# Regrouping the products with V in a fused attention, routing and gated-convolution kernel

## The chip, the cores and the metric

The kernel runs on one core of one Trainium2 chip. The metric is device time in microseconds (us) of one execution; less is better. The engines named below are PE (TensorE: matmuls and transposes), ACT (ScalarE), DVE (VectorE), POOL (GpSimd) and SP (SyncE, which issues nearly all of the DMAs here). Each runs its own instructions in program order and waits for the others through semaphores.

## The reference, cut to what matters

Three stages follow each other. Only the first, clustered attention over 2 batches, 8 heads, 768 positions and 64 channels a head, is touched.

```python
def _attn_ref(q, k, v, centroids):
    scale = 1.0 / np.sqrt(D)
    q_assign = np.argmax(np.einsum('bhsd,hcd->bhsc', q_n, c_n), axis=-1)
    k_assign = np.argmax(np.einsum('bhsd,hcd->bhsc', k_n, c_n), axis=-1)
    mask = q_assign[:, :, :, None] == k_assign[:, :, None, :]
    scores = scale * np.matmul(q, k.transpose(0, 1, 3, 2))
    scores = np.where(mask, scores, -1000000000.0)
    scores = scores - np.max(scores, axis=-1, keepdims=True)
    attn = np.exp(scores)
    attn = attn / (np.sum(attn, axis=-1, keepdims=True) + 1e-09)
    return np.matmul(attn, v).astype(np.float32)
...
x = _moe_ref(x=x, **moe_kwargs)      # each token goes through one of 8 experts
return _moe2_ref(x=x, **moe2_kwargs) # causal convolution gate, value product, output product
```

## The kernel before, in words

The attention handles 8 pairs of heads (`g` 0 to 7). A pair has two query blocks of 384 queries (`u` counts the blocks, 0 to 15), and a block has six items: 3 tiles of 128 queries times 2 heads. So there are 96 items and one loop over them, written out in program order; this text calls one pass of it a **trip**, and counts the trips of a pair 0 to 11 (`i % 12`; `j` is 0 to 5 within a block). Nothing reorders the instructions: each engine does its share of each trip in the order of the code.

A trip `i` does, in this order:

- `do_S(i + 2)` (L658): four PE matmuls make the scores of item `i + 2` in one of the **two** buffers of `ps_s` (tile `s`), and DVE takes the row maximum (`mx`, L675). The buffer is the one that item `i` used, so these matmuls wait until ACT has read it, that is for the exponential of item `i`.
- `do_T(i)` (L689): six PE transposes of item `i`'s exponentials, in two halves (`tp`, two buffers), each copied to SBUF (`pt`). In the trips 2, 3, 4, 5, 6 and 9 of a pair ACT copies both halves (L704); in the others DVE copies one (L702).
- `do_exp(i + 2)` (L678): the exponential on ACT (L684), once the maximum is there.
- the **products with V** (`do_PV`, L706) of the block before: six key tiles, two matmuls each (one for each head, 64 columns wide), added up in `pv`. They come in groups of two key tiles, in the trips `j` = 1, 3 and 5. After the last, ACT copies `pv` (`post1`, L718).
- a step of the **preparation of the next pair** (`prep_steps`, L369). `k_hi` and `q_hi` (ACT), `k_lo` (POOL) and `q_lo` (DVE) split keys and queries into a high and a low part in tile `xx`; `dots1` (PE: `dott`, then DVE: `dsb`) and `dots2` (PE: `dots`) make the products with the cluster centres; `argmax1` to `argmax4` (DVE, POOL) find each position's cluster; `rows` (PE: `pr`) and `rows_out` (ACT: `ohr`) turn it into one-hot rows. `stack1` (three SP DMAs a head, `st<-xx`) and `stack2` (two a head, `st<-ohr`) lay it all into `st`, from which the scores of the next pair are made from trip 10 on. The list has six steps, done in the trips 0 to 5 of a pair; in the first pair (which prepares the second) in the trips 1 to 6.
- in `j` = 3 (`j` = 4 in the pairs 4 and 5) `post2` (L725) of the block before the last: three PE products (`po`) and four small DVE operations. In the pairs 4 and 5 the trips 6 to 9 also hold steps of the routing of tokens (`route_steps`, L518), with a scan on DVE (`r3`) between two PE steps (`r2p`, `r3p`).

The first block has no products with V, since there is no block before it, and the last block (`u` 15) does them in two groups of three already, in its first two trips. Trip 7 of the first pair also holds nine small DVE operations of `conv_weights`.

Of the kernel before, what the change touches and what calls it, by code (L numbers as in the profile page):

```python
# [8 lines left out]
F32 = mybir.dt.float32  # L9
# [32 lines left out]
def routed_attention_moe_kernel(  # L42
# [12 lines left out]
    nc = tc.nc  # L55
# [58 lines left out]
    def keep_warm(ps, n):  # L114

        for _ in range(n):
            nc.tensor.matmul(ps, onesb, onesb.unsqueeze(1).to_broadcast([128, 4, 128]), start=True, stop=True)
# [251 lines left out]
    def prep_steps(g):  # L369
        b, p = pairs[g]  # L370
        x = X[g]
        xx = xx_p.tile([128, 4, S], F32R, tag="xx", name="xx")
# [72 lines left out]
            nc.scalar.activation(ohr, pr, AF.Identity, bias=rowb[:, 1:2], scale=rowb[:, 0:1])  # L445
            o["ohr"] = ohr

        def stack1(h):
            s = st[h]
            r = slice(64 * h, 64 * h + 64)  # L450
            nc.sync.dma_start(s[0:64, 0:2, :].bitcast(F32), xx[r, 0:2, :].bitcast(F32))
            nc.sync.dma_start(s[64:128, 0:2, :].bitcast(F32), xx[r, 0:3:2, :].bitcast(F32))
            nc.sync.dma_start(s[0:64, 2:4, :].bitcast(F32), xx[r, 1:4:2, :].bitcast(F32))

        def stack2(h):
            r = o["ohr"].bitcast(F32)
            nc.sync.dma_start(st[h][64:80, 2, :].bitcast(F32), r[32 + 16 * h:48 + 16 * h, :])
            nc.sync.dma_start(st[h][64:80, 3, :].bitcast(F32), r[16 * h:16 * h + 16, :])

        def S0(h, parts=None):  # L460

            if parts:
                S_[h] = ps_s.tile([128, 2, 512], F32, tag="s", name="s")
                r = slice(64 * h, 64 * h + 64)
                for n, (a, c) in enumerate(parts):
                    for m in range(2):
                        nc.tensor.matmul(
                            S_[h][:, m, :384], xx[r, a, 0:128], xx[r, c, 384 * m:384 * m + 384],
                            start=(n == 0), stop=False,
                        )  # L470
            else:
                for m in range(2):
                    nc.tensor.matmul(
                        S_[h][:, m, :384], st[h][64:80, 2, 0:128], st[h][64:80, 3, 384 * m:384 * m + 384],
                        start=False, stop=True,
                    )
                row_max(h, S_[h])

        def rows0(h):
            for i in range(2):  # L480
                pl, tag = ((ps_t, "t"), (ps_v, "pv") if i else (ps_m, "m"))[h]
                pr = pl.tile([128, 1024], BF16, tag=tag, name="pr0")
                for t in range(NQT):
                    c = 8 * (t % 3) + 4 * (t // 3) + 2 * i + h
                    nc.tensor.transpose(pr[64:80, 128 * t:128 * t + 128], o["oh"][:, c, :], identb)
                if i:
                    nc.scalar.copy(st[h][64:80, 2, :], pr[64:80, :S])
                else:
                    nc.vector.tensor_scalar(
                        st[h][64:80, 3, :], pr[64:80, :S], NEG, -NEG, op0=ALU.mult, op1=ALU.add  # L490
                    )

        if g == 0:
            return [[
                cent_norm, k_hi, k_lo, q_hi, dots1, dots2, q_lo,
                lambda: nc.scalar.activation(warm[:, 1:2], warm[:, 0:1], AF.Exp),
                lambda: S0(0, ((1, 0), (1, 3), (2, 0))), lambda: S0(1, ((1, 0), (1, 3), (2, 0))),
                lambda: keep_warm(ps_v.tile([128, 512], F32, tag="pv", name="spin1"), 2),
                lambda: stack1(0), lambda: stack1(1),
                argmax1, argmax2, argmax3, argmax4, lambda: rows0(0), lambda: rows0(1), lambda: S0(0), lambda: S0(1),  # L500
            ]]
        return [
            [k_hi, dots1],
            [q_hi, k_lo, dots2],
            [argmax1, argmax2],
            [q_lo, lambda: stack1(0), lambda: stack1(1)],
            [argmax3, argmax4],
            [rows, rows_out, lambda: stack2(0), lambda: stack2(1)],
        ]

# [147 lines left out]
    def do_S(i):  # L658
        g, qb, t, h = items[i]
        st = ST[g][h]  # L660
        q0 = 384 * qb + 128 * t
        ps = ps_s.tile([128, 2, 512], F32, tag="s", name="s")
        for n in range(2):
            nc.tensor.matmul(  # L664
                ps[:, n, :384], st[:, 1, q0:q0 + 128], st[:, 0, 384 * n:384 * n + 384], start=True, stop=False
            )
        for n in range(2):
            nc.tensor.matmul(  # L668
                ps[:, n, :384], st[0:80, 2, q0:q0 + 128], st[0:80, 3, 384 * n:384 * n + 384], start=False, stop=True
            )  # L670
        row_max(i, ps)
# [6 lines left out]
    def do_exp(i):  # L678
        g, qb, t, h = items[i]
        ps, mx = S_.pop(i)  # L680
        if (t, h) == (0, 0):
            Zt[i // 6] = small.tile([128, 3, 2], F32, tag="z", name="z", bufs=4)
        pt = p_p.tile([128, 2, 384], F32, tag="p", name="pexp", bufs=3)
        nc.scalar.activation(  # L684
            pt, ps[:, :, :384], AF.Exp, bias=mx[:, 0:1], accum_out=Zt[i // 6][:, t, h:h + 1]
        )
        P_[i] = pt.rearrange("p a b -> p (a b)")

    def do_T(i, act_only):  # L689
        g, qb, t, h = items[i]  # L690
        u = i // 6
        if t == 0:
            PT[u, h] = pt_p.tile([128, NQT, 384], F32, tag=f"pt{h}", name=f"pt{h}")
        p = P_.pop(i)
        for half in range(2):
            tp = ps_t.tile([128, 3, 128], F32, tag="t", name="tp")
            for k in range(3):
                kt = 3 * half + k
                nc.tensor.transpose(tp[:, k, :], p[:, 128 * kt:128 * kt + 128], ident)  # L699
            dst = PT[u, h][:, 3 * half:3 * half + 3, 128 * t:128 * t + 128]  # L700
            if half == 0 and not act_only:
                nc.vector.tensor_copy(dst, tp)  # L702
            else:
                nc.scalar.copy(dst, tp)  # L704

    def do_PV(u, kt):  # L706
        g, qb = items[6 * u][:2]
        if kt == 0:
            PVs[u] = ps_v.tile([128, 384], F32, tag="pv", name="pv")
        for h in range(2):  # L710
            nc.tensor.matmul(  # L711
                PVs[u][64 * h:64 * h + 64, :], Vt[g][:, kt, h, :], PT[u, h][:, kt, :],
                start=(kt == 0), stop=(kt == NQT - 1), skip_group_check=True,
            )
# [108 lines left out]
    for i in range(NI):  # L823
        g, qb, t, h = items[i]
        u, j = divmod(i, 6)
        if i % 12 == 0:
            prep = prep_steps(g + 1) if g + 1 < 8 else []
        if i + 2 < NI:
            do_S(i + 2)
        do_T(i, act_only=i % 12 in (2, 3, 4, 5, 6, 9) or u >= U - 1)  # L830
        if i + 2 < NI:
            do_exp(i + 2)
        if u == U - 1:
            if j < 2:
                for kt in range(3):
                    do_PV(u - 1, 3 * j + kt)
            if j == 1:
                post1(u - 1)
        elif u and j % 2:
            for kt in (j - 1, j):  # L840
                do_PV(u - 1, kt)
            if j == 5:
                post1(u - 1)
        ps = i % 12 - (0 if g else 1)
        if 0 <= ps < len(prep):
            for f in prep[ps]:
                f()
        if i in (54, 66):
            route = route_steps(i // 12 - 4)
        if j == (0 if u == U - 1 else 4 if i // 12 in (4, 5) else 3) and u > 1:  # L850
            post2(u - 2)
        if i == 6 * U - 4:
            post2(u - 1)
            route = route_steps(2)
        if 6 <= i % 12 <= 9 and i // 12 in (4, 5) or 2 <= j and u == U - 1:
            for _ in range((1, 3, 2, 3)[i % 12 - 6 if i // 12 in (4, 5) else j - 2]):
                route.pop(0)()
        if u == U - 1 and j >= 2:
            if j in (2, 4):
                last_PV(j // 2 - 1)  # L860
        if i % 12 == 8 and g + 2 < 8:
            load_kq(g + 2)
        if i % 12 == 7 and 0 < g < 7:
            load_v(g + 1)
        if g and i % 12 in (0, 1, 10, 11):
            next(fill, None)
        if i == 7:
            conv_weights()
        if i == 82:
            w_whole(0, ring0)  # L870
        if i == 86:
            w_whole(1, ring0, "lo")
        if i == 90:
            w_whole(2, wstg, "w")
        if i == 84:
            early_load()
        if i == 89:
            early_rows()
# [723 lines left out]
```

## Time and profile before

| what | value |
|---|---|
| median of 3 runs | 529.61 us (528.85 to 531.57) |
| the profiled execution | 530.8 us, its span 528.7 us |
| PE busy | 509.7 us, 96% of the span |
| DVE, ACT, POOL busy | 361.6, 312.8 and 95.0 us |
| mean granted TensorE clock | 0.984 of full speed |
| chain that ended last | PE 41%, DMA 4%, every other engine 1% or less |

The span runs from the first to the last profiled instruction; the execution's own time holds some 2 us around it. The loop over items fills the stretch from 18 us to about 250 us. A busy PE counts a matmul from its start to its modelled end, so neighbouring matmuls overlap, and a short wait of PE's can hide under the end of the matmul before. Steps are therefore measured below from the start of one group of instructions to the start of the next.

### The profile page before, as it was taken

What the parts mean: (1) busy time and instruction counts of PE and PEld (TensorE: products, weight loads), DVE (VectorE), ACT (ScalarE), POOL (GpSimd) and SP (SyncE); (2) the same over time, 40 slices, a digit from 0 to 9 for tenths busy, and PEclk for the clock granted to TensorE, in tenths of its full rate; (3) what the DMA queues carried; (4) which work ended last, traced back from release to release, by engine and by line L of the source; (5) the groups of instructions that cost most, each with busy time, mean ns of one, the idle gap of its engine ahead of it and who ended that gap; (6) DMA issues with size and microseconds to landing.
All of it is one profiled execution on the core that took longest, in us unless ns stands there. A gap on an engine that the chain in (4) does not pass through costs nothing. (4 is left out here: it accounts for less than half of the span.)

```text
span 528.7 us, 8832 instructions
## 1 busy us (share of the span) xinstructions
PE 509.7 (96%) x3189; PEld 405.7 (77%) x3190; DVE 361.6 (68%) x704; ACT 312.8 (59%) x597; POOL 95.0 (18%) x106
## 2 busy tenths in 40 slices
PE   7898999999999999999989899999999999999996
PEld 3675767777676777776859788979898886899885
DVE  6684767665687787554726489996875791599960
ACT  3596867777777767766332356645435373485642
POOL 5111002020103022000220003424435252000000
PEclk7899999999999999999999799999999999999999
DMA  5877687888977883840459945886999846730023
GB/s 146 232 150 225 140 263 207 220 260 197 316 161 267 203 263 79 235 172 0 111 192 338 349 119 194 282 301 226 365 326 349 310 156 234 235 136 2 20 100 119
DMA packets 35352, 108.38 MB, mean 205 GB/s; under 512 B 4666, under 2 KB 5178, under 8 KB 30697
## 3 DMA queue, kind: packets, MB, share of 16 engines
q1 hardware_dynamic: 32217, 100.90, 62.2%
q0 software_dynamic: 2128, 6.31, 3.2%
q10 hardware_dynamic: 960, 0.58, 0.4%
q8 instruction: 26, 0.43, 0.3%
q14 instruction: 21, 0.17, 0.1%
HBM read 58.14 MB, written 29.58 MB: 166 GB/s over the span
## 5 line engine op out<-in xcount | busy, mean ns | idle before, releaser
L675 DVE TENSOR_REDUCE mx<-s 128x1 f32<-128x768 f32 x96 | 91.5, 954 | 59.8 <-PE s L668 53.6
L704 ACT COPY pt<-tp 128x384 f32<-128x384 f32 x148 | 65.5, 482 | 55.8 <-PE tp L699 55.7
L684 ACT ACTIVATE pexp<-s,mx 128x768 f32<-128x768 f32 x96 | 87.0, 906 | 6.6 <-DVE mx L675 5.1
L699 PE MATMUL tp<-ident,pexp 128*128 128x128 f32 x576 | 80.8, 276 | 0.3 <-DVE pt L702 0.2
L699 PEld LDWEIGHTS tp<-ident,pexp 128*128 128x128 f32 x576 | 67.8, 141 | 7.7 <-ACT pt L704 3.3
L711 PE MATMUL pv<-pt,vt 128*64 128x384 f32 x360 | 67.8, 498 | 0.0
L366 DVE TENSOR_TENSOR wlo<-wraw,whi 128x1024 fp32r<-128x1024 f32 x40 | 55.4, 1393 | 11.7 <-ACT whi L360 11.4
L664 PE MATMUL s<-st 128*128 128x384 f32 x188 | 57.6, 388 | 1.7 <-ACT pexp L684 1.7
L668 PE MATMUL s<-st 80*128 80x384 f32 x188 | 48.8, 341 | 1.4 <-DMA st<-ohr 1.4
L1163 PE MATMUL hps<-xhi,wone 128*128 128x176 f32 (+3 forms) x320 | 48.4, 312 | 0.0
L1163 PEld LDWEIGHTS hps<-xhi,wone 128*128 128x128 f32 x320 | 46.9, 197 | 1.2 <-ACT xhi L1132 0.2
L360 ACT CAST whi<-wraw 128x1024 fp32r<-128x1024 f32 x40 | 40.6, 1044 | 10.0 <-PE yp L1200 5.1
L664 PEld LDWEIGHTS s<-st 128*128 128x128 f32 x188 | 28.8, 192 | 18.0 <-issue 7.3
L711 PEld LDWEIGHTS pv<-pt,vt 128*64 128x64 f32 x360 | 21.9, 136 | 23.8 <-issue 23.8
L1170 ACT ACTIVATE h<-hps 128x352 fp32r<-128x352 f32 (+6 forms) x36 | 16.2, 450 | 38.6 <-PE hps L1163 38.5
L668 PEld LDWEIGHTS s<-st 80*128 80x128 f32 x188 | 34.5, 191 | 1.7 <-issue 1.7
L1198 PE MATMUL yp<-whi,h 128*112 128x512 f32 (+5 forms) x88 | 34.9, 397 | 0.9 <-ACT h L1170 0.9
L384 POOL TENSOR_TENSOR xx<-xkq,xx 128x768 fp32r<-128x768 f32 x8 | 14.6, 1820 | 116.4 <-ACT xx L378 95.9
L1199 PE MATMUL yp<-wlo,h 128*112 128x512 f32 (+5 forms) x88 | 34.7, 394 | 0.0
L1200 PE MATMUL yp<-whi,h 128*112 128x512 f32 (+5 forms) x88 | 34.6, 394 | 0.0
L1423 DVE SCALAR_TENSOR_TENSOR gt<-xf,convw_sb,gt 128x768 f32<-128x768 f32 x32 | 31.9, 1013 | 0.4
L1206 ACT ACTIVATE ysb<-yp,pw 64x512 f32<-64x512 f32 (+6 forms) x16 | 11.0, 685 | 33.8 <-PE yp L1196 17.0
(280 smaller groups left out, 911.2 us busy)
## 6 DMA issues: line engine op xcount, KB each, us to landing
wraw<-in_wq_dram SPq DMA_DIRECT2D x20, 1024.0 KB
st<-xx SPq DMA_DIRECT2D x48, 384.0 KB
wone<-in_wq_dram SPq DMA_DIRECT2D x12, 1024.0 KB
xslots<-padrow SPq DMA_DIRECT2D x15, 771.0 KB
xkq<-in_kq_dram SPq DMA_DIRECT2D x15, 384.0 KB
wspace<-in_wd_dram SPq DMA_DIRECT2D x8, 512.0 KB
xall<-xnat SPq DMA_DIRECT2D x4, 771.0 KB
vt<-in_v_dram SPq DMA_DIRECT2D x8, 384.0 KB
```

What stands on the lines that cost most here:

```text
L360: nc.scalar.copy(hi[:, c], wraw[j][:, c])
L366: nc.vector.tensor_tensor(lo[:, c], t[:, c], hi[:, c].bitcast(F32), op=ALU.subtract)
L664: nc.tensor.matmul(ps[:, n, :384], st[:, 1, q0:q0 + 128], st[:, 0, 384 * n:384 * n + 384], start=True, stop=False)
L668: nc.tensor.matmul(ps[:, n, :384], st[0:80, 2, q0:q0 + 128], st[0:80, 3, 384 * n:384 * n + 384], start=False, stop=True)
L675: nc.vector.tensor_reduce(mx, ps[:, :, :384], axis=AX.XY, op=ALU.max, negate=True)
L684: nc.scalar.activation(pt, ps[:, :, :384], AF.Exp, bias=mx[:, 0:1], accum_out=Zt[i // 6][:, t, h:h + 1])
L699: nc.tensor.transpose(tp[:, k, :], p[:, 128 * kt:128 * kt + 128], ident)
L704: nc.scalar.copy(dst, tp)
L711: nc.tensor.matmul(PVs[u][64 * h:64 * h + 64, :], Vt[g][:, kt, h, :], PT[u, h][:, kt, :], start=(kt == 0), stop=(kt == NQT - 1), skip_grou ...
L1163: nc.tensor.matmul(hp, a[:, d, fs], c[:, d, :w], start=(n + d == 0), stop=(n + d == len(terms) + 2))
L1198: nc.tensor.matmul(yp[:r], h[:, fa, hi], whv[:, f, :], start=(q == 0 and f == 0), stop=False)
L1199: nc.tensor.matmul(yp[:r], h[:, fa, hi], wlv[:, f, :], start=False, stop=False)
```

## The change

The products with V are done in two groups of three key tiles, in the trips `j` = 0 and 3, and `post1` follows in `j` = 3. An empty step is put into the list of the pairs from the third on, so that `rows`, `rows_out` and `stack2` come in trip 6 instead of 5. For the second pair (prepared in the first, trips 1 to 6) `q_hi` and `k_lo` come one step sooner, `q_lo` too, and two of head 0's three `stack1` DMAs are issued two steps sooner, its third and head 1's in the step in which they were.

```diff
+        def stack1(h, parts=(0, 1, 2)):
             s = st[h]
             r = slice(64 * h, 64 * h + 64)
...
+            for n in parts:
+                dst = (s[0:64, 0:2, :], s[64:128, 0:2, :], s[0:64, 2:4, :])[n]
+                src = (xx[r, 0:2, :], xx[r, 0:3:2, :], xx[r, 1:4:2, :])[n]
+                nc.sync.dma_start(dst.bitcast(F32), src.bitcast(F32))
...
+        if g == 1:
+            return [
+                [k_hi, q_hi, k_lo, dots1],
+                [dots2, lambda: stack1(0, (0, 2))],
+                [argmax1, argmax2, q_lo],
+                [lambda: stack1(0, (1,)), lambda: stack1(1)],
+                [argmax3, argmax4],
+                [rows, rows_out, lambda: stack2(0), lambda: stack2(1)],
+            ]
         return [
             [k_hi, dots1],
             [q_hi, k_lo, dots2],
             [argmax1, argmax2],
             [q_lo, lambda: stack1(0), lambda: stack1(1)],
             [argmax3, argmax4],
+            [],
             [rows, rows_out, lambda: stack2(0), lambda: stack2(1)],
         ]
...
-        elif u and j % 2:
-            for kt in (j - 1, j):
+        elif u and j % 3 == 0:
+            for kt in range(j, j + 3):
                 do_PV(u - 1, kt)
-            if j == 5:
+            if j == 3:
                 post1(u - 1)
```

What this moves on the engines is shown at three places. First PE in the second pair, its trips 7 and 8 before (`s` are scores, `tp` transposes, `pv` products with V):

```order
L664 MATMUL s<-st_331 128x384 x2
L668 MATMUL s<-st_331 128x384 x2
L699 MATMUL tp<-ident,pexp 128x128 x6
L711 MATMUL pv<-pt_651,vt 64x384
L711 MATMUL pv<-pt_683,vt 64x384
L711 MATMUL pv<-pt_651,vt 64x384
L711 MATMUL pv<-pt_683,vt 64x384
L664 MATMUL s<-st_330 128x384 x2
L668 MATMUL s<-st_330 128x384 x2
L699 MATMUL tp<-ident,pexp 128x128 x6
```

and the same trips, with trip 9 behind them, after:

```order
L675 MATMUL s<-st_331 128x384 x2
L679 MATMUL s<-st_331 128x384 x2
L710 MATMUL tp<-ident,pexp 128x128 x6
L675 MATMUL s<-st_330 128x384 x2
L679 MATMUL s<-st_330 128x384 x2
L710 MATMUL tp<-ident,pexp 128x128 x6
L675 MATMUL s<-st_331 128x384 x2
L679 MATMUL s<-st_331 128x384 x2
L710 MATMUL tp<-ident,pexp 128x128 x6
L722 MATMUL pv<-pt_651,vt 64x384
```

Two trips now stand side by side with no products with V in or between them; before, no such trips were neighbours outside of the first block. (The lines of the changed kernel are 11 higher from here on.)

Second PE at the start of the second pair, trips 0 and 1, where the third pair's products with the cluster centres are made, before:

```order
L699 MATMUL tp<-ident,pexp 128x128 x6
L396 MATMUL dott<-xkq,cd 32x384 x4
L664 MATMUL s<-st_331 128x384 x2
L668 MATMUL s<-st_331 128x384 x2
L699 MATMUL tp<-ident,pexp 128x128 x6
L711 MATMUL pv<-pt_486,vt 64x384
```

and after, from the last product with V of trip 0:

```order
L722 MATMUL pv<-pt_526,vt 64x384
L396 MATMUL dott<-xkq,cd 32x384 x4
L675 MATMUL s<-st_331 128x384 x2
L679 MATMUL s<-st_331 128x384 x2
L710 MATMUL tp<-ident,pexp 128x128 x6
L406 MATMUL dots<-ident,dsb 128x128 x3
```

`dott` has moved from behind transposes to behind products with V, and `dots` the other way; trip 1 has lost its products with V.

Third DVE in the first pair, around `q_lo` of the second pair (the row that writes `xx`), before:

```order
L675 TENSOR_REDUCE mx<-s 128x1 x2
L414 TENSOR_REDUCE amx<-dots 128x24
L419 TENSOR_TENSOR eq<-dots,amx 128x384
L675 TENSOR_REDUCE mx<-s 128x1
L387 SCALAR_TENSOR_TENSOR xx<-xkq,xx 128x768
L675 TENSOR_REDUCE mx<-s 128x1
```

and after:

```order
L686 TENSOR_REDUCE mx<-s 128x1 x2
L414 TENSOR_REDUCE amx<-dots 128x24
L419 TENSOR_TENSOR eq<-dots,amx 128x384
L387 SCALAR_TENSOR_TENSOR xx<-xkq,xx 128x768
L686 TENSOR_REDUCE mx<-s 128x1 x2
```

`q_lo` has moved ahead of one row maximum, that of item 6.

## Rows read from the trace of the kernel before

**Rows 1.** Windows: length, then busy us (instructions) of each engine, granted clock, DMA
```profile
25.90:33.40 7.50, 7.01 (x49) 5.72 (x47) 6.70 (x10) 7.50 (x19) 2.24 (x4) 1.00 0.43 86
...
47.27:76.75 29.48, 29.48 (x199) 21.24 (x197) 19.53 (x32) 21.99 (x48) 2.83 (x2) 1.00 0.74 196
...
225.82:240.16 14.34, 14.34 (x96) 10.55 (x95) 7.68 (x14) 10.20 (x25) 0.00 (x0) 1.00 0.30 125
```

**Rows 2.** Timeline, second pair, PE, trips 6 to 9: start, us, what
```profile
62.70 0.62 PE L664 MATMUL s<-st 128*128 128x384 f32 x2
...
64.09 0.59 PE L664 MATMUL s<-st 128*128 128x384 f32 x2
...
65.62 1.51 PE L711 MATMUL pv<-pt,vt 128*64 128x384 f32 x8
...
67.06 0.62 PE L664 MATMUL s<-st 128*128 128x384 f32 x2
...
69.26 0.90 PE L699 MATMUL tp<-ident,pexp 128*128 128x128 f32 x6
```

**Rows 3.** Timeline, last block, PE: `po`, then a trip with a group of three key tiles
```profile
243.78 1.01 PE L736 MATMUL po<-wgl_sb,ut 128*128 128x146 f32 x6
244.53 0.61 PE L664 MATMUL s<-st 128*128 128x384 f32 x2
...
248.17 0.61 PE L664 MATMUL s<-st 128*128 128x384 f32 x2
```

**Rows 4.** Timeline, third pair, PE, trip 0, which starts at 76.75
```profile
77.56 0.82 PE L699 MATMUL tp<-ident,pexp 128*128 128x128 f32 x6
78.31 0.85 PE L396 MATMUL dott<-xkq,cd 128*32 128x384 f32 x8
79.09 0.62 PE L664 MATMUL s<-st 128*128 128x384 f32 x2
```

**Rows 5.** Timeline, DVE and ACT: maximum and exponential of the scores begun at 62.70
```profile
63.78 0.96 DVE L675 TENSOR_REDUCE mx<-s 128x1 f32<-128x768 f32 x1 [1.89 <-PE s L668]
...
64.85 0.91 ACT L684 ACTIVATE pexp<-s,mx 128x768 f32<-128x768 f32 x1
```

**Rows 6.** Timeline, first block, ACT and PE, trips 5 and 6 (no products with V)
```profile
28.70 0.92 ACT L684 ACTIVATE pexp<-s,mx 128x768 f32<-128x768 f32 x1
...
29.77 0.62 PE L664 MATMUL s<-st 128*128 128x384 f32 x2 [0.34 <-ACT pexp L684]
...
31.41 0.62 PE L664 MATMUL s<-st 128*128 128x384 f32 x2
```

**Rows 7.** Timeline, third pair, ACT and PE: `q_hi` and `dots` in trip 1
```profile
82.10 0.55 PE L406 MATMUL dots<-ident,dsb 128*128 128x128 f32 x3
82.12 0.84 ACT L381 ACTIVATE xx<-xkq 128x768 fp32r<-128x768 f32 x1
...
82.40 0.59 PE L664 MATMUL s<-st 128*128 128x384 f32 x2
```

**Rows 8.** Timeline, pair 4, DVE and PE: the scan `r3` and `r3p`
```profile
156.58 0.92 DVE L556 TENSOR_TENSOR_SCAN sc<-rps,zrow 1x384 f32<-1x384 f32 x1
...
157.65 0.34 PE L564 MATMUL rps<-ident,sc 1*128 1x1 f32 x3
```

**Rows 9.** Timeline, first pair: DVE around `q_lo` and `conv_weights`, SP, PE
```profile
28.92 0.95 DVE L675 TENSOR_REDUCE mx<-s 128x1 f32<-128x768 f32 x1
...
29.78 1.11 DVE L387 SCALAR_TENSOR_TENSOR xx<-xkq,xx 128x768 fp32r<-128x768 f32 x1
...
37.44 0.18 DVE L305 TENSOR_TENSOR convw_sb<-ctop,cw 128x20 f32<-128x20 f32 x1
...
39.47 1.71 SPq L458 DMA_DIRECT2D st<-ohr  x1
...
42.93 0.59 PE L668 MATMUL s<-st 80*128 80x384 f32 x2 [1.38 <-DMA st<-ohr]
...
43.93 0.59 PE L664 MATMUL s<-st 128*128 128x384 f32 x2
```

More of the change, by code (lines that the diff above doesn't have):

```diff
@@ L446, in rows_out @@
             o["ohr"] = ohr
-        def stack1(h):
+        def stack1(h, parts=(0, 1, 2)):
             s = st[h]
             r = slice(64 * h, 64 * h + 64)
-            nc.sync.dma_start(s[0:64, 0:2, :].bitcast(F32), xx[r, 0:2, :].bitcast(F32))
-            nc.sync.dma_start(s[64:128, 0:2, :].bitcast(F32), xx[r, 0:3:2, :].bitcast(F32))
-            nc.sync.dma_start(s[0:64, 2:4, :].bitcast(F32), xx[r, 1:4:2, :].bitcast(F32))
+            for n in parts:
+                dst = (s[0:64, 0:2, :], s[64:128, 0:2, :], s[0:64, 2:4, :])[n]
+                src = (xx[r, 0:2, :], xx[r, 0:3:2, :], xx[r, 1:4:2, :])[n]
+                nc.sync.dma_start(dst.bitcast(F32), src.bitcast(F32))
         def stack2(h):
```

## The prediction

> **What bounds the kernel now.** I read the windows first [rows 1]. In the second pair, 47.27 to 76.75 us, PE is busy 29.48 of 29.48 us, DVE 19.5 and ACT 22.0; so PE sets the pace, at a granted clock of 1.00 (the 2.4 GHz level), and the other engines have some 30% of room on the mean. The window 25.90 to 33.40 lies in the first block, where there are no products with V, and there it is different: ACT is busy 7.50 of 7.50 us and PE 7.01, still at clock 1.00. So which engine sets the pace depends on how the products with V are spread over the trips. Next I read the timeline of PE from group to group [rows 2 to 4, 6], and of DVE and ACT beside it [rows 5, 6], for the chain that a trip must let finish.
>
> **What a group of products with V costs.** A plain trip (scores and transposes) lasts 64.09 - 62.70 = 1.39 us; one with two key tiles 67.06 - 64.09 = 2.97, so two tiles cost 1.58 [rows 2]. A trip with three tiles, in the last block, lasts 248.17 - 244.53 = 3.64 [rows 3], so three cost 2.25. The third tile costs 0.67, and each group has 1.58 - 1.34 = 0.24 that doesn't grow with the tiles. Three groups of two are 4.74 us a block, two of three 4.50: the change saves 0.24 in each of 14 blocks, 3.4 us in all.
>
> This rule of the Trainium skill speaks for the change: TensorEngine Tiling (Array Packing), Tiling Modes, says that going from one tiling mode to another drains the engine, and products 64 columns wide stand here among full ones. The trace agrees, with the 0.24 just worked out; by that rule alone the whole change would save those 3.4 us and lose nothing.
>
> **What moving `dott` and `dots` costs.** In trip 0 the transposes start 77.56 - 76.75 = 0.81 after the scores, so in a plain trip they hold PE for 0.58; `dott` starts 0.75 after them [rows 1, 4]: a pause of 0.17. Behind products with V that pause should fall away, since they have paid it: between 0 and 0.17 saved a pair, I take 0.17. `dots` costs 82.40 - 82.10 = 0.30 [rows 7] in either place. So PE's own work falls by 2 x 0.24 + 0.17 = 0.65 us a pair.
>
> **What two plain trips side by side cost.** This is the term that decides. The scores begun in a trip need the buffer of the scores two trips earlier. From the start of scores to the start of their maximum are 63.78 - 62.70 = 1.08 us, from there to the start of the exponential 64.85 - 63.78 = 1.07 [rows 2, 5], and from there to the scores that take the buffer over, where PE did wait for it, 29.77 - 28.70 = 1.07 [rows 6]. That is 3.22 us, so two trips in a row can't last less. Today every second trip holds products with V, and two trips last 1.39 + 2.97 = 4.36. After the change the trips 1-2, 4-5, 7-8 and 10-11 of a pair are without them, and two plain trips are 2.78 of PE: a wait of **0.44 us** at the next trip's scores. The first block bears this out: there a trip lasts 31.41 - 29.77 = 1.64 [rows 6], half of 3.28.
>
> Trips 4-5, 7-8 and 10-11 so lose 0.44 each. Trips 1-2 hold `dots`, 3.08 us, and lose 0.14 by this; but `q_hi` (0.84 on ACT [rows 7]) now lies in a trip of 1.7 us instead of 3.3, ahead of the copies that free the transposes' buffers. Between 0 and 0.84 of it comes through to PE; I take half, 0.42. The sum of waits is 1.88 a pair. From it goes 0.16: in two trips a pair the transposes already take 0.90 instead of 0.82 [rows 2, 4], the same kind of wait. Net for a pair: 1.88 - 0.65 - 0.16 = +1.07, and for the four pairs 1, 2, 3 and 6 **+4.3**.
>
> In the pairs 4 and 5 `po` stands in trips 4 and 10 (244.53 - 243.78 = 0.75 [rows 3]), which lifts those couples to 3.53, over the 3.22, and the routing steps do so for trips 7-8. But `r3p` waits there: the scan (0.92 [rows 8]) comes behind the maximum of trip 7, which ends 1.08 + 0.96 = 2.04 after that trip's scores [rows 2, 5], and behind a copy and three small operations, for which I allow 1.0; so `r3p` can't start before 3.9 or 4.0, and PE is there after two trips and `r2p`, some 3.2. Today `r3p` starts at once after its transposes, since products with V lie in between. Between 0 and 0.8; I take 0.75. Per pair -0.65 + 0.14 + 0.42 + 0.75 = +0.66, for both **+1.3**.
>
> The half pair before the last block has one regrouped block and two couples, of which the second holds the early transposes: -0.24 + 0.44 = **+0.2**.
>
> **The first pair.** PE now stands for 1.38 us at 42.93 until `st<-ohr` has landed, and the next trips are disturbed: trip 11 lasts 47.27 - 43.93 = 3.34 instead of 2.97 [rows 1, 2, 9]. With the copies of head 0 issued sooner, SP, which issued the last of its rows at 39.47 [rows 9], is through with `st<-xx` earlier, while the scores of trip 10 come later; so I take the whole 1.38 + 0.37 as gone, and 0.24 for one block. Against that, `q_lo` (1.11) goes ahead of the maximum that started at 28.92: that starts at 30.03, its exponential at 31.10, and the scores that need its buffer at 32.17 instead of 31.41 [rows 6, 9]: 0.76. The couples 7-8 and 10-11 lose 0.44 each. And the nine operations of `conv_weights` (0.18 each [rows 9], 1.6 in all), which lay in a trip with products with V, now hold up the maximum and a copy in plain trips: between 0 and 1.6, I take 0.7. The sum is -1.99 + 2.34 = **+0.3**, between -0.7 and +1.3.
>
> No work is hidden at no cost elsewhere: the one-hot rows move a trip later, but behind trip 6 there are still two plain trips, a wait and a full trip, 1.39 + 1.39 + 0.44 + 3.64 + 0.75 = 7.6 us, before the scores of trip 10 read them.
>
> **Sum.** 4.3 + 1.3 + 0.2 + 0.3 = +6.1 us, all ahead of the routing, so that everything behind shifts with it: 530.8 + 6.1 = 536.9 for an execution like the profiled one. That one lay 1.2 above the median of the runs shown, so the time is 535.7.
>
> **The rivals.**
> - *Faster.* The waits don't come, since ACT and DVE enter a plain couple idle after a trip of 3.6 to 4.4 us. For it speaks that they are idle 30% on the mean [rows 1]; against it, that the 3.22 us hold no queue, just three latencies one after the other. It decides if the chain were 2.78 or less. Then 3.4, 6 x 0.17 = 1.0 and 1.75 of the first pair are saved, 6.1 in all: 530.8 - 6.1 - 1.2 = 523.5. This is also what the drain rule above comes to. Chance 0.06.
> - *No change.* The waits come at a third: 0.65 a pair would be eaten exactly if each of the three lone couples lost 0.15 and `q_hi` nothing more. The time would be about 529.6. The first block's 1.64 a trip [rows 6] speaks against it, but there ACT was full, and here it has caught its breath. Chance 0.13.
> - *Much slower.* The one-hot rows come too late in every pair, and the wait of 1.38 [rows 9] appears seven times: 8.3 more than the sum (six further pairs), 544. Against it the 7.6 us above. Chance 0.05.
> - The forecast, 0.76.
>
> **How the numbers follow.** If each of the roughly fourteen lone waits were 0.15 less or more, the sum moves by 2.1; `q_hi` at its ends by 2.5, `r3p` by 1.5 down, the first pair by 1. Together some 4 us either way: 531.7 to 539.7 holds the forecast and part of both neighbours. Half a per cent, 2.6 us, is about what this kernel's runs tell from no change. Slower than 532.3 is the forecast, less a small tail, and the much slower case: 0.80; within it 0.14; faster 0.06.
>
> **What the changed profile would show.** Right: in the pairs 1, 2, 3 and 6 a period of about 30.5 instead of 29.48 us, and waits of PE's scores for ACT's `pexp` in the trips 0, 3, 6 and 9, where none stand now; groups of 12 `pv` records in two trips a block; no wait for `st<-ohr`. Wrong: a period of 28.7 or less, so that the chain is shorter than I read it; or waits for `st<-ohr` in every pair; or a granted clock below 1.00 in the attention.

## The result, and the profile after

| | before | after |
|---|---|---|
| median of 6 runs each | 530.16 us (528.18 to 531.57) | 535.29 us (534.3 to 535.77) |
| the profiled execution, its span | 530.8 us, 528.7 us | 535.29 us, 533.3 us |
| PE busy | 509.7 us (96%) | 509.1 us (95%) |
| mean granted clock | 0.984 | 0.987 |

The ratio after to before is 1.0095, with a 95% interval of 1.0069 to 1.0122: slower by about 1%. Two runs, one of the kernel before (1003 us) and one of experiment 4 (569 us), were far slower than the others of their kernel and stay out of the ratios. PE is busy for the same time to 0.6 us while the span is 4.6 us longer, so it waits more.

These are the windows of the changed kernel for the second pair, pair 4 and the half pair ahead of the last block (columns as in [rows 1]: length, then the busy us of PE, of PEld, which loads PE's weights, of DVE, ACT and POOL, granted clock, DMA share, GB/s):

```profile
47.91:78.15 30.24, 29.82 (x198) 21.38 (x198) 19.56 (x33) 22.20 (x48) 2.83 (x2) 1.00 0.63 159
138.64:169.12 30.48, 29.76 (x207) 22.13 (x208) 22.74 (x59) 22.31 (x49) 4.64 (x4) 1.00 0.84 233
231.16:245.55 14.39, 14.32 (x95) 10.71 (x95) 8.02 (x14) 9.86 (x23) 0.00 (x0) 1.00 0.27 113
```

The second pair lasted 29.48 us, all of it busy PE [rows 1]; now it lasts 30.24 and PE shows 0.42 idle, with the clock at 1.00 (2.4 GHz) as before. Idle time shows only part of the loss, because matmuls overlap; from start to start, trips 0 to 11 of this pair last (an ordinary table, read from the timelines):

```
trip      0    1    2    3    4    5    6    7    8    9    10   11
before  2.34 3.31 1.36 3.72 1.38 3.31 1.39 2.97 1.39 3.84 1.38 3.09   sum 29.48
after   4.42 1.71 1.46 4.80 1.37 1.76 3.98 1.38 1.79 4.40 1.38 1.79   sum 30.24
```

Two neighbouring trips without products with V (1-2, 4-5, 7-8, 10-11) are called a plain couple here. The second of each (trips 2, 5, 8, 11) is 0.1 to 0.4 longer than a plain trip, and trip 3 is longer than trip 9. The timeline of the couple 4-5, PE, DVE and ACT, shows why (start, us, what, and in brackets the idle time before it and who ended it):

```profile
60.31 0.60 PE L675 MATMUL s<-st 128*128 128x384 f32 x2
...
61.30 0.96 DVE L686 TENSOR_REDUCE mx<-s 128x1 f32<-128x768 f32 x1
61.63 0.86 ACT L715 COPY pt<-tp 128x384 f32<-128x384 f32 x2 [1.48 <-PE tp L710]
...
61.68 0.60 PE L675 MATMUL s<-st 128*128 128x384 f32 x2
...
62.38 0.92 ACT L695 ACTIVATE pexp<-s,mx 128x768 f32<-128x768 f32 x1
...
63.44 0.30 PEld L675 LDWEIGHTS s<-st 128*128 128x128 f32 x2 [0.39 <-ACT pexp L695]
63.44 0.62 PE L675 MATMUL s<-st 128*128 128x384 f32 x2
```

The scores begun at 60.31 hold their buffer until the exponential that starts at 62.38 has read it; the scores at 63.44 take it over. That is 0.99 + 1.08 + 1.06 = 3.13 us for two trips that have 2.75 of PE work, so 0.38 is lost. The PE row itself carries no bracket; the wait is on the weight loader's row, since the transposes' modelled end covers most of it on PE.

The waits of the weight loader in the pairs 1 to 3 (us in total, times, longest), two lines of the view:

```profile
PEld s L675 <- ACT pexp L695: 3.0, 9, 0.4
PEld tp L710 <- ACT pt L715: 2.5, 9, 0.5
```

The first did not stand in the same stretch before, and it comes nine times, three a pair, at the scores of the trips 6, 9 and 0; the 0.1 lost ahead of trip 3 is not listed. Of the second, three waits, of 0.45, come from `q_hi`; the other six, of 0.19, stand in the trips 8 and 11. In trip 3 of the second pair, ACT and PE:

```profile
55.36 0.83 ACT L381 ACTIVATE xx<-xkq 128x768 fp32r<-128x768 f32 x1
...
55.51 0.62 PE L675 MATMUL s<-st 128*128 128x384 f32 x2
...
56.09 0.85 ACT L715 COPY pt<-tp 128x384 f32<-128x384 f32 x2
...
56.61 0.69 PEld L710 LDWEIGHTS tp<-ident,pexp 128*128 128x128 f32 x6 [0.45 <-ACT pt L715]
56.61 0.93 PE L710 MATMUL tp<-ident,pexp 128*128 128x128 f32 x6
```

`q_hi` stands ahead of the copies that free the transposes' buffers; trip 3's transposes start 56.61 - 55.51 = 1.10 after their scores instead of 0.8.

By pair, the change in length is +0.62 (first), +0.76, +0.78, +0.58 (pairs 1 to 3), +0.25, +0.91 (4, 5), +1.41 (6) and +0.05 (the half pair): +5.4 at the end of the windows, 240.16 before [rows 1] and 245.55 now, and +4.6 in the whole span.

### The profile page after: what moved, and what is told of

It reads as the page before. It is cut to its first block, busy times and chain, and to the rows that moved or that the text cites. A ratio compares the mean times of both kernels' runs of the same rounds, so it can differ in the third digit from the quotient of the medians.

```text
span 533.3 us, 8832 instructions
## 1 busy us (share of the span) xinstructions
PE 509.1 (95%) x3189; PEld 406.3 (76%) x3190; DVE 361.7 (68%) x704; ACT 313.7 (59%) x597; POOL 95.8 (18%) x106
## 5 line engine op out<-in xcount | busy, mean ns | idle before, releaser
L710 PE MATMUL tp<-ident,pexp 128*128 128x128 f32 x576 | 81.9, 277 | 2.4 <-DVE pt L713 1.2
L722 PE MATMUL pv<-pt,vt 128*64 128x384 f32 x360 | 64.7, 495 | 0.0
L722 PEld LDWEIGHTS pv<-pt,vt 128*64 128x64 f32 x360 | 23.1, 136 | 26.5 <-issue 26.5
```

The source lines that it names most:

```text
L722: nc.tensor.matmul(PVs[u][64 * h:64 * h + 64, :], Vt[g][:, kt, h, :], PT[u, h][:, kt, :], start=(kt == 0), stop=(kt == NQT - 1), skip_grou ...
```

## The experiments

The theory is the prediction's: the plain couples (waits for the scores' buffer) and `q_hi` in a short trip cost more than the saved groups bring. One rival is that the new lists cost it, another that groups of three cost PE something themselves. All runs are compared with the kernel before on the same chip. A period is the length of a pair from scores to scores; the numbers of the pairs 1 to 3 are given, where nothing but attention and preparation runs.

**1. The groups without the new lists.** The kernel before with this alone:

```diff
-        elif u and j % 2:
-            for kt in (j - 1, j):
+        elif u and j % 3 == 0:
+            for kt in range(j, j + 3):
...
-            if j == 5:
+            if j == 3:
```

> Only the two groups of three; the preparation lists are those of before. Wait theory (what costs is the wait of the scores behind two plain trips): the one-hot rows stand in trip 5 again and fill the couple 4-5 to 1.38 + 1.38 + 0.43 = 3.19 us, just what the chain needs, so the 0.38 there go, and the waits of 0.41 behind the couples 7-8 and 10-11 and the 0.40 of the transposes in trip 3 stay: pairs 1, 2 and 3 at about 29.85 us (changed kernel 30.24, before 29.48), the whole some 2 to 4 us slower than before, ratio 1.005 to 1.008. Rival 1 (the moved list steps and copies cost the time): pairs at 28.6 to 28.9, ratio 0.993 or less. Rival 2 (groups of three cost PE more than groups of two): periods as in the changed kernel, ratio 1.009.

Measured: 536.39 us, ratio 1.0149 (1.0106 to 1.0192); periods 30.30 to 30.36. So it is the regrouping that costs, and the lists, which the one rival blames, win some of it back. By the periods alone the run came out as the second rival had it. The trips speak against that one: a trip with a group of three lasts 3.64 here (trip 6), as it did in the last block of the kernel before [rows 3], so such a group costs PE no more than the prediction took for it. The period was expected at 29.85, with the one-hot rows filling a couple, and that was a miss. Trip 5 of the second pair, PE and DVE:

```profile
61.91 0.60 PE L664 MATMUL s<-st 128*128 128x384 f32 x2
...
62.70 0.82 PE L699 MATMUL tp<-ident,pexp 128*128 128x128 f32 x6
62.98 0.56 DVE L429 TENSOR_TENSOR oh<-wts,arr 128x384 bf16<-128x384 f32 x1
63.60 0.52 PE L435 MATMUL pr<-identb,oh 128*64 128x128 bf16 x6
...
64.05 0.61 PE L664 MATMUL s<-st 128*128 128x384 f32 x2
```

The rows' products stand in the couple, but they wait until DVE has made `oh`, and trip 5 lasts 64.05 - 61.91 = 2.14, trip 6 3.64, together 5.78; with the rows in trip 6 the same two last 1.76 + 3.98 = 5.74. So they fill nothing: one wait stands where another would. The empty step is worth only some 0.1 in these pairs; in the pairs 4 and 5 it is worth 0.8 (31.29 and 31.97 here, 30.48 and 31.16 with it).

**2. The lists without the groups.** The changed kernel with the products with V in three groups of two again.

```diff
-        elif u and j % 3 == 0:
-            for kt in range(j, j + 3):
+        elif u and j % 2:
+            for kt in (j - 1, j):
...
-            if j == 3:
+            if j == 5:
```

> Only the lists: second pair's steps and copies sooner, one-hot rows a trip later; products with V in three groups of two as before. Wait theory: no two plain trips are neighbours, so pairs 1, 2, 3 and 6 stay at 29.48 within 0.1; the first pair loses its 1.38 us wait for the one-hot copies or most of it and pays up to 0.76 for the maximum behind q_lo: 0 to 1.5 us faster in all, ratio 0.997 to 1.000. Rival 1 (the lists cost the time): pairs near 30.2, ratio 1.008.

Measured: 528.85 us, ratio 0.9993 (0.9965 to 1.002): no change. The periods are 29.78 to 29.79, so 0.3 worse where 0.1 was allowed: rows made behind transposes cost 0.62, those behind products with V 0.33. The first pair wins 1.16 (28.08 instead of 29.24): no wait for `st<-ohr` any more, but a new one, which the changed kernel has too. PE in the first pair:

```profile
32.18 0.62 PE L675 MATMUL s<-st 128*128 128x384 f32 x2 [1.16 <-ACT pexp L695]
```

**3 and 4. The chain shortened.** Both kernels without the row maximum (this part of the computation is left out: the exponentials are taken of the scores as they are), and with the transposes' copies all on DVE, which that frees; of the kernel before (3) and of the changed one (4):

```diff
     def row_max(i, ps):
-        mx = small.tile([128, 1], F32, tag="mx", name="mx", bufs=4)
-        nc.vector.tensor_reduce(mx, ps[:, :, :384], axis=AX.XY, op=ALU.max, negate=True)
-        S_[i] = ps, mx
+        S_[i] = ps, nomx
...
-            if half == 0 and not act_only:
-                nc.vector.tensor_copy(dst, tp)
-            else:
-                nc.scalar.copy(dst, tp)
+            nc.vector.tensor_copy(dst, tp)
```

> The kernel before with the row maximum left out (the exponential takes the scores without it) and all copies of transposes on DVE, so that the exponential can follow the scores at once: the chain from scores to the buffer's next scores is about 1.05 + 1.07 = 2.1 us instead of 3.2. Wait theory: PE bounds the kernel before anyway, so pairs go from 29.48 to about 29.3 (only the 0.08 in two trips go), ratio 0.997 to 1.000. Rival 2 says the same.

> The changed kernel with the same two things done: no row maximum, copies on DVE. Wait theory: two plain trips (2.76) now cover the chain (2.1), so the waits in trips 0, 3, 6 and 9 go and the sign turns: pairs at about 28.5 to 28.7, 0.7 to 0.9 less than the kernel before treated alike, the whole 4 to 7 us faster than it, ratio to the kernel before 0.985 to 0.990. Rivals 1 and 2 (the lists, or the groups themselves): still 4 to 5 us slower than the kernel before treated alike, ratio 1.006 or more.

Measured: 529.79 us for 3 (ratio 1.0005, 0.9975 to 1.0034; periods 29.25, 29.25 and 29.86, the last with a `dott` that waited for a load) and 526.7 for 4 (ratio 0.9933, 0.9898 to 0.9968; periods 29.00). The sign of the change turns: with the long chain a period is 0.76 longer by it, with the short one 0.25 shorter. Of the whole time this shows less: the medians differ by 3.1 us, but from the start of the second pair to the last block the traces of 3 and 4 last 192.0 and 191.4 us (before and after the change 192.9 and 197.6), as the pairs 4 and 5 are 0.63 and 0.73 longer in 4. So the cost is gone, but most of the 3.1 is not the couples'. PE and DVE in the changed kernel without the maximum, from trip 5 on:

```profile
60.88 0.59 PE L677 MATMUL s<-st 128*128 128x384 f32 x2
...
62.24 0.59 PE L677 MATMUL s<-st 128*128 128x384 f32 x2
62.35 0.56 DVE L431 TENSOR_TENSOR oh<-wts,arr 128x384 bf16<-128x384 f32 x1
...
62.83 1.02 DVE L712 COPY pt<-tp 128x384 f32<-128x384 f32 x2
...
63.44 1.01 PE L710 MATMUL tp<-ident,pexp 128*128 128x128 f32 x6 [0.26 <-DVE pt L712]
```

Trips 5, 8 and 11 last 1.35 to 1.37 (62.24 - 60.88 = 1.36): the couples are whole. Period 29.00 was above the 28.5 to 28.7 expected, and the ratio above its 0.985 to 0.990, in part because the edit has a wait of its own: trip 6 lasts 4.55 instead of 3.97, since the copies, now all on DVE, stand behind `argmax3` and `argmax4` (whose last operation makes `oh`). That groups of three cost PE more than groups of two falls with this too.

**5. One tile in every trip.** If couples are the trouble, products with V in all six trips should have no wait, and cost three times the fixed part more than two groups.

```diff
-        elif u and j % 2:
-            for kt in (j - 1, j):
-                do_PV(u - 1, kt)
+        elif u:
+            do_PV(u - 1, j)
```

> The kernel before, its lists too, but one key tile of the products with V in every trip (six groups of one a block). No trip is plain, so no wait behind a couple can arise. Wait theory with the fixed cost of 0.24 us a group: three more groups a block, 0.72 more, less the pause that dott no longer pays (0.17 a pair) and the 0.08 in two trips: pairs at about 30.6 instead of 29.48, the whole about 8 us slower, ratio 1.013 to 1.018. Rival (a group has no cost of its own, and only waits count): pairs at 29.3, ratio 0.995 to 1.000.

Measured: 541.66 us, ratio 1.018 (1.013 to 1.0231); periods 31.12 to 31.17, where about 30.6 was expected. PE, from trip 7 on:

```profile
65.96 0.62 PE L664 MATMUL s<-st 128*128 128x384 f32 x2
...
67.52 0.87 PE L711 MATMUL pv<-pt,vt 128*64 128x384 f32 x4
68.32 0.62 PE L664 MATMUL s<-st 128*128 128x384 f32 x2
```

A trip with one tile lasts 68.32 - 65.96 = 2.36, so the tile costs 2.36 - 1.39 = 0.97; with 0.67 for the tile itself the fixed part is 0.30, more than the 0.24 of the prediction; twelve such groups a pair at 0.06 more each cover the 0.5 by which the period was off. There is a real price per group, and the change does save it.

**6. `q_hi` out of the couple.** The changed kernel with `q_hi` one step sooner for the pairs from the third on:

```diff
-            [k_hi, dots1],
-            [q_hi, k_lo, dots2],
+            [k_hi, q_hi, dots1],
+            [k_lo, dots2],
```

> The changed kernel with q_hi (ACT, 0.83 us) of the pairs from the third on put into trip 0, beside products with V, instead of the plain trip 1. Wait theory: trip 3 falls from 4.80 to 4.40, since its transposes no longer wait for copies that ACT does after q_hi; pairs from 30.24 to 29.84; the whole some 2.4 us less than the changed kernel, ratio to before 1.004 to 1.006. Rival (the 0.40 in trip 3 come from the maximum or the one-hot steps on DVE): trip 3 stays at 4.80, ratio 1.009.

Measured: 533.22 us, ratio 1.0048 (1.0022 to 1.0074); periods 29.83 to 29.85. PE, trip 3 of the second pair:

```profile
56.07 0.62 PE L675 MATMUL s<-st 128*128 128x384 f32 x2
...
56.88 0.82 PE L710 MATMUL tp<-ident,pexp 128*128 128x128 f32 x6
57.63 2.16 PE L722 MATMUL pv<-pt,vt 128*64 128x384 f32 x12
...
60.47 0.61 PE L675 MATMUL s<-st 128*128 128x384 f32 x2
```

The transposes come 0.81 after their scores again, and trip 3 lasts 60.47 - 56.07 = 4.40 as trip 9 does. Over six pairs this one move is 2.4 us.

**7. The couples filled.** The groups of three kept, and PE work that needs nothing late put into the second trip of each couple: the one-hot rows in trip 5 (with `argmax3` and `argmax4` in trip 3, two steps ahead of them, so that they don't wait as in experiment 1), the `po` products of one block in trip 7 and of the other in trip 10; `q_hi` as in 6; the transposes' copies in the trips 8 and 11 on ACT; in the pairs 4 and 5 rows and `po` stay where they were and the routing's `r3p` stands ahead of trip 9's products with V; in the first pair `q_lo` back behind the maximum and `conv_weights` in trip 9.

```diff
-            [k_hi, dots1],
-            [q_hi, k_lo, dots2],
+            [k_hi, q_hi, dots1],
+            [k_lo, dots2],
             [argmax1, argmax2],
-            [q_lo, lambda: stack1(0), lambda: stack1(1)],
-            [argmax3, argmax4],
+            [q_lo, lambda: stack1(0), lambda: stack1(1), argmax3, argmax4],
             [],
+            *([[]] if g in (5, 6) else []),
             [rows, rows_out, lambda: stack2(0), lambda: stack2(1)],
...
+                late = {1: [u - 3], 4: [u - 2]}.get(j, []) if qb else []
+            for n in late:
+                post2(n)
...
-        if i == 7:
+        if i == 9:
             conv_weights()
```

> Two groups of three as in the change, but no couple of plain trips is left empty: the one-hot rows stand in trip 5, po of the first block in trip 7 of its pair, po of the second in trip 10; q_hi in trip 0, the last argmax steps in trip 3, ACT copies all transposes in the trips 8 and 11 too; in the pairs 4 and 5 po stays in trips 4 and 10, the rows in trip 6, and r3p comes just ahead of the products with V of trip 9; in the first pair q_lo goes back behind the maximum of item 6 and conv_weights into trip 9. Wait theory: pairs 1, 2, 3 and 6 at 28.9 (before 29.48), 4 and 5 at 29.2 (30.23), the whole 5 to 7 us faster than before, ratio 0.987 to 0.991. Rival 1 (the lists) and rival 2 (the groups themselves) leave it slower than before, 1.004 or more.

Measured: 523.8 us (523.26 to 524.98), ratio 0.9873 (0.9842 to 0.9905): faster than both kernels. Windows of its second pair and of pair 4, and PE in the trips 5 and 6 of the second pair:

```profile
46.12:74.88 28.76, 28.76 (x198) 21.49 (x198) 17.89 (x30) 22.62 (x50) 2.84 (x2) 1.00 0.72 190
132.50:161.84 29.34, 29.34 (x210) 22.18 (x209) 22.85 (x58) 23.04 (x52) 4.63 (x4) 1.00 0.86 248
```

```profile
58.67 0.59 PE L675 MATMUL s<-st 128*128 128x384 f32 x2
...
60.20 0.52 PE L435 MATMUL pr<-identb,oh 128*64 128x128 bf16 x6
60.65 0.62 PE L675 MATMUL s<-st 128*128 128x384 f32 x2
```

PE is busy the whole of both windows, and trip 5 lasts 60.65 - 58.67 = 1.98 with the rows in it, against 1.76 with nothing but a wait. The trips of the second pair are 4.42, 1.72, 1.39, 3.65, 1.38, 1.98, 3.65, 2.11, 1.37, 3.62, 2.11 and 1.37: what was a wait of 0.4 is now work that another trip has lost. Of the 6.1 us won over the kernel before, 1.15 are won ahead of the second pair, which starts at 46.12 instead of 47.27.

**8. Only the maximum left out.** As 4 (the row maximum left out), but with the copies where the changed kernel has them.

> The changed kernel with the row maximum left out and nothing else: the copies of the transposes stay where they were, ahead of the exponential on ACT. If the chain is scores, maximum, exponential alone, the waits behind the couples go and pairs fall to about 29.0. If a second path of equal length (transposes, their copies on ACT, then the exponential, some 2.1 us after the scores as well) holds them, pairs stay at 30.0 to 30.3. I expect the second.

Measured, in a single run: 525.43 us, with periods of 30.01 and 30.02. The couples 4-5, 7-8 and 10-11 still wait. PE and ACT in the couple 4-5:

```profile
57.63 0.61 PE L677 MATMUL s<-st 128*128 128x384 f32 x2
...
58.96 0.86 ACT L715 COPY pt<-tp 128x384 f32<-128x384 f32 x2 [1.49 <-PE tp L710]
...
59.01 0.59 PE L677 MATMUL s<-st 128*128 128x384 f32 x2
...
59.70 0.92 ACT L695 ACTIVATE pexp<-s,nomx 128x768 f32<-128x768 f32 x1
...
60.77 0.62 PE L677 MATMUL s<-st 128*128 128x384 f32 x2
```

The exponential needs no maximum now and the scores that it reads were begun at 57.63, but it starts at 59.70, 0.74 after ACT began the copies ahead of it in its order. So there are two paths of nearly equal length to the exponential of a couple: by the maximum (62.38 - 60.31 = 2.07 after the scores in the changed kernel) and by the transposes and their copies on ACT (59.70 - 57.63 = 2.07 here). Taking one away leaves the other; experiment 4 took both, by moving the copies as well. (Trip 5 stays at 1.76; in the trips 8 and 11, where DVE makes one of the two copies, 1.79 fell to 1.71.)

That the whole time is 9.9 us less than the changed kernel's all the same is not the couples' doing. By the spans it is 9.5: 2.6 in the first pair, 0.7, 1.3 and 0.9 in the pairs 4, 5 and 6, where waits behind DVE's maximum went or shrank (`r3p`'s trip 8 lasts 1.84 for 2.45, trip 0 of pair 6 4.41 for 5.06), some 0.2 in each of the pairs 1 to 3, and 3.2 behind the attention, which no run explains. The kernel before was not run with the maximum alone left out, so what that gains without the regrouping is not known; the couples are judged by their trips.

## Why the prediction was right, and where its terms were off

**The mechanism stands.** Of the three ways to remove the waits, each moved the periods as waits of this size would: shortening both paths turned the sign (4 against 3), moving `q_hi` took its own 0.40 (6), and filling the couples gave a kernel faster than both (7). A third buffer for the scores, which would test the wait by itself, was not tried. The rivals fall with the same runs: that the waits don't come, by the nine waits for `pexp`; that they come at a third, by their size (the rival's own sum does not close either: three times 0.15 and the 0.14 are 0.59, not 0.65); that the one-hot rows come late, since the changed kernel waits for `st<-ohr` in no pair.

**PE's own work per group.** 0.24 was worked out from two and three tiles; one tile gives 0.30. What the change saves of PE is seen where its waits are taken off: the second pair is 0.76 longer with 0.09 + 0.40 + 0.38 + 0.41 + 0.41 = 1.69 of waits, so 0.93 was saved, where 0.65 + 0.16 = 0.81 was forecast. Most of the other 0.12 are the waits that went with the old spacing, taken as 0.08 in two trips but 0.12 in size: trips 9 and 11 of before last 3.84 and 3.09 where trips 3 and 7, with the same work, last 3.72 and 2.97, and without these waits the period is 0.23 shorter (experiment 3). The rule that the prediction weighed (the Trainium skill, TensorEngine Tiling (Array Packing), Tiling Modes) is that going to another tiling mode drains the engine. These runs agree with it in that each group has a price of 0.24 to 0.30; that a drain is its cause no run shows, and that the waits outweigh it is outside of what the rule states.

**The waits.** Forecast 0.44 behind each lone couple, measured 0.38 to 0.41: the chain is 3.13 in the couple 4-5 and 3.17 in the two others, not 3.22; in the couple 4-5 scores, maximum and exponential follow each other in 0.99, 1.08 and 1.06 instead of 1.08, 1.07 and 1.07. The couple with `dots` lost 0.1 (forecast 0.14), `q_hi` 0.40 (forecast 0.42, taken as half of 0 to 0.84, a guess that came near by luck). Together 1.69 for 1.88. The chain was only one of two paths, as experiment 8 shows; the prediction named one, and that the result is the same because they are equally long is luck too.

**The pairs 1, 2, 3 and 6.** Forecast +4.3, measured +3.5 (0.76 + 0.78 + 0.58 + 1.41). The two terms above make it less; against them a wait of 0.62 came in trip 0 of the pairs 5 and 6 that was not foreseen. DVE and PE at the start of pair 6:

```profile
200.06 0.55 DVE L754 TENSOR_TENSOR xnat<-po,rz 128x384 f32<-128x384 f32 x1
...
200.53 0.95 DVE L686 TENSOR_REDUCE mx<-s 128x1 f32<-128x768 f32 x1
...
201.40 0.55 DVE L713 COPY pt<-tp 128x384 f32<-128x384 f32 x1
...
202.00 0.55 PE L710 MATMUL tp<-ident,pexp 128*128 128x128 f32 x3 [0.35 <-DVE pt L713]
```

In the pairs 4 and 5 `po` stands in trip 10, and its multiplications (`xnat`) and a maximum now stand on DVE right ahead of trip 11's copy, in a plain trip. The copy comes at 201.40 and trip 0's second transposes wait for it. The prediction counted `po` as work that lifts the couple over the chain, and not what DVE does behind it.

**The pairs 4 and 5.** Forecast +1.3, measured +1.2, and that is luck. `r3p` cost 2.45 - 1.81 = 0.64 in trip 8 (forecast 0.75), and the savings were larger than forecast here too, so pair 4 is only 0.25 longer where 0.66 was forecast; pair 5 comes to 0.91 by the 0.62 above, which was not foreseen.

**The first pair.** Forecast +0.3, measured +0.6. But 0.8 of that is trip 1, whose products with the centres waited for a load that lies ahead of everything that was changed (with the same lists, those of before, this trip lasts 3.61 in the kernel before, 5.08 in experiment 1 and 3.56 in experiment 5), so the change itself brought -0.2, inside the -0.7 to +1.3 given. Near the forecast it comes by luck, since its waits and its savings were both larger. Its waits as the trace after shows them, PE and DVE:

```profile
24.25 0.84 PE L396 MATMUL dott<-xkq,cd 128*32 128x384 f32 x6 [0.78 <-DMA xkq<-in_kq_dram]
...
32.68 0.62 PE L675 MATMUL s<-st 128*128 128x384 f32 x2 [1.17 <-ACT pexp L695]
...
39.83 0.62 PE L675 MATMUL s<-st 128*128 128x384 f32 x2
...
40.68 0.18 DVE L305 TENSOR_TENSOR convw_sb<-ctop,cw 128x20 f32<-128x20 f32 x1
40.77 0.95 DVE L686 TENSOR_REDUCE mx<-s 128x1 f32<-128x768 f32 x1
41.64 0.55 DVE L713 COPY pt<-tp 128x384 f32<-128x384 f32 x1
...
42.25 0.55 PE L710 MATMUL tp<-ident,pexp 128*128 128x128 f32 x3 [0.85 <-DVE pt L713]
...
44.81 0.62 PE L675 MATMUL s<-st 128*128 128x384 f32 x2
```

`q_lo` ahead of the maximum gives 1.17 (0.76 forecast), and `conv_weights`, whose last operation starts at 40.68, holds a maximum and a copy up: PE stands idle for 0.85, and trip 9 lasts 44.81 - 39.83 = 4.98, 1.33 more than the 3.65 of experiment 7, where `conv_weights` comes later (0.7 forecast). The wait of 1.38 for `st<-ohr` is gone, as forecast; trip 4, which the forecast does not name, is 0.69 shorter as well (2.37 with the lists of before, in experiment 1 too, 1.69 with the new ones, in experiment 2 too).

**The half pair.** Forecast +0.2, measured +0.05.

**The sum.** Forecast +6.1 for the whole, measured +5.4 at the end of the attention and +4.6 at the end. The prediction said that everything behind shifts by the same; 0.8 did not. Part of it is seen in the timeline of PE at the transposes of the first expert's tokens, before:

```profile
276.75 0.43 PE L1126 MATMUL xp<-ident,xs 64*128 64x64 f32 x4 [0.55 <-DMA xs<-xslots]
```

and after:

```profile
281.72 0.43 PE L1137 MATMUL xp<-ident,xs 64*128 64x64 f32 x4 [0.20 <-DMA xs<-xslots]
```

They waited 0.55 for the gathered tokens and now wait 0.20: the transfers between did not come later by as much as PE did. The rest, some 0.45, is given back behind the first expert's transposes, where the granted clock was 0.95 from 300 to 350 us before and 0.97 from 305 to 355 after; no run tested whether that is the cause. That the time still came within 0.4 us of the forecast is luck in part: the medians are 5.1 apart, 1.0 less than the 6.1, while the median of before, taken as 529.6 from three runs, is 530.2 over six.

## What to carry to other kernels

Before regrouping work on the bounding engine, work out the shortest time in which that engine's buffers can come round (here 3.1 to 3.2 us for two trips) and compare it with the work that each stretch of so many trips holds afterwards; a busy share of 100% says nothing about it, since the old spacing may be what hides it. When waits appear, fill them with work whose inputs are long ready, and move ahead of them what stands in front of the copies, as in experiments 6 and 7: the saving was there, 6 us of it, once the couples were filled. Look for the second path of equal length before shortening the first.

## What was not expected of the hardware

- The fixed price of a group of 64-column products among full ones is not a constant: 0.30 us for a group of one key tile, 0.24 worked out from groups of two and three, with 0.67 for a tile in both.
- The same six `pr` products (64 columns, bf16) cost 0.62 us of trip time behind transposes and 0.33 behind products with V, which are 64 columns wide too (experiment 2).
- With one and the same kernel the span follows the mean granted clock of the run only loosely: of experiment 4, 521.8 us at 1.00 and 527.5 at 0.981, yet 523.1 at 0.987 and 525.9 at 0.996. A single profile of each kernel can't settle a difference of half a per cent.
